# Softmax sums: adding four exponential tiles into one with accumulating transfers

## The chip, the cores and the metric

One core of a Trainium2 chip runs the kernel. The metric is the device time in microseconds of one execution; the median of several executions is given. The profile is of one execution of its own.

## The reference

Attention with an RMS norm on queries and keys, then two matrix products with a leaky ReLU between them. There are 8 batches, 12 heads, 448 positions and a head dimension of 64; the second part has 3584 rows, widths 768 and 2048.

```python
q_n, k_n = (rmsnorm(q, g_q), rmsnorm(k, g_k))
scores = scale * np.matmul(q_n, k_n.transpose(0, 1, 3, 2))
scores = scores - np.max(scores, axis=-1, keepdims=True)
attn = np.exp(scores)
attn = attn / (np.sum(attn, axis=-1, keepdims=True) + 1e-09)
return np.matmul(attn, v).astype(np.float32)
# with x = the above, its heads put side by side:
h = x @ w_in
g = np.maximum(0.01 * h, h)
return (g @ w_out).astype(np.float32)
```

## The kernel before, in words

The attention is cut into 24 units: unit u is four heads of one batch, three units to a batch. The key positions of a unit are cut into seven tiles. For each tile t, `score` (L195) writes the transposed scores to PSUM, keys on the partitions and the 448 queries along a row, and `ex` (L214, ScalarE) writes their exponentials as fp16 to the tile `et[:, t]`: 128 partitions, each with two rows of 448, 224 KB in all.

Since keys lie on partitions, the softmax sum of a query is a sum over partitions and over the seven tiles. For units 4 to 22 (`narrow`) TensorE does it in `zcol` (L283): a matrix of ones and zeros, 128 by 32, is the stationary operand, and each tile takes four matmuls of 224 columns that write four different groups of 32 PSUM partitions. Seven tiles accumulate in the same bank, 28 matmuls. From the sums ScalarE makes the inverse (`zcol_ln` L300, `zcol_inv` L305), four transfers of SyncE spread it over the partitions (L310, tile `rz`), and GpSimd multiplies it with the unit's unscaled output (`xmul_pool`, L320), for units up to 7 VectorE. `pv_out` (L295, ScalarE) has copied that output from PSUM to `x32`, of which there is one buffer.

The order of the work is written out by hand; each engine runs its instructions in that order. The main loop goes over the units, and each unit has four steps d = 0 to 3, which compute key tiles 0; 1 and 2; 3 and 4; 5 and 6. In step 0 of unit u TensorE does the scores of tile 0, then for unit u-1 the product with v (`pv_slot`, L340) and `zcol`, then `shift_mm` (L244), a small matmul that takes the maximum of unit u over partitions; VectorE made its input `dg` (L234) just before. L245 and L253 on VectorE turn it into the bias `eb` that every exponential of the unit needs. On ScalarE, `pv_out` of unit u-1 stands ahead of the first exponential of u.

The rest of each step is filled by `fill` from a queue of work on the two matrix products of earlier batches (L362, L403, L444, L564); the queue is spread so that it is empty when the next batch is ready. `load` brings q and k for unit u+4 on SyncE's queue. GpSimd's queue carries in step 0 the load of v for unit u+3 (`load_v`, L124), which waits for the end of unit u-1's product, and in step 1 `xmul_pool` of unit u-1.

Of the kernel before, what the change touches and what calls it, by code (L numbers as in the profile page):

```python
# [8 lines left out]
FP32 = mybir.dt.float32  # L9
FP16 = mybir.dt.float16  # L10
AF = mybir.ActivationFunctionType
ALU = mybir.AluOpType
# [6 lines left out]
def kernel(  # L19
# [11 lines left out]
    nc = tc.nc  # L31

    B, H, S, D = q.shape
    QH = 4
    NS = 7
    P = 128
    NQ = H // QH
    NU = B * NQ
# [6 lines left out]
    cst = ctx.enter_context(tc.tile_pool(name="cst", bufs=1))  # L45
# [4 lines left out]
    zpool = ctx.enter_context(tc.tile_pool(name="zpool", bufs=1))  # L50
# [6 lines left out]
    def aux(shape, dtype, name):  # L57
        if held:
            return held[0].pop(0)
        return psum.tile(shape, dtype, tag="aux", bufs=4, name=name)  # L60
# [6 lines left out]
    def drop(bank):  # L67
        if held:
            held[0].append(bank)
# [5 lines left out]
    onesr = cst.tile([P, 32], FP16)  # L75
# [6 lines left out]
    nc.vector.memset(eps_t, 1.0e-6)  # L82
    one32 = cst.tile([1, 1], FP32)
    nc.vector.memset(one32, 1.0)
    grow = cst.tile([1, 2, D], FP32)
    gdup = cst.tile([1, 2, D], FP32)
    gcol = cst.tile([P, 1], FP32)
    gate_t = cst.tile([P, 1], FP16)
    vts = [cst.tile([P, 2, NS, D], FP16, name=f"vt{i}") for i in range(NV)]
# [21 lines left out]
    st = {}  # L111
# [11 lines left out]
    def load_v(u):  # L123
        nc.gpsimd.dma_start(vts[u % NV].rearrange("p a t d -> p a (t d)"), rows(v, u))  # L124
# [9 lines left out]
    def buf(u, name):  # L134
        if name not in st[u]:
            shape, dtype, bufs = SHAPES[name]
            st[u][name] = prep_p.tile(shape, dtype, tag=name[:2] if bufs == 3 and name != "qkT" else name, bufs=bufs, name=name)
        return st[u][name]
# [7 lines left out]
    def prep_sqp(u, tis=BOTH):  # L146
        for ti in tis:
            nc.gpsimd.tensor_tensor(buf(u, f"sq{ti}"), raw[u][ti], raw[u][ti], op=ALU.mult)
# [49 lines left out]
    def qk(u, steps):  # L198
        st[u]["sT"] = []
        for t in steps:  # L200
            sT = slot()
            score(u, t, (sT[:, 0], sT[:, 1]))
            st[u]["sT"].append((t, sT))
# [17 lines left out]
    def shift_max(u):  # L221
        s = st[u]
        sT = s["sT"][0][1]
        if isinstance(sT, list):
            pm2 = small.tile([P, 2], FP32, tag="pm2", name="pm2")
            for a in range(2):
                nc.vector.tensor_reduce(pm2[:, a:a + 1], sT[a][:, 0:S], axis=AXL.X, op=ALU.max)
            s["spare"] = sT[0]
            nc.vector.tensor_reduce(s["spare"][:, 511:512], pm2, axis=AXL.X, op=ALU.max)
        else:  # L230
            s["spare"] = sT[:, 0]
            nc.vector.tensor_reduce(s["spare"][:, 511:512], sT[:, :, 0:S], axis=AXL.XY, op=ALU.max)  # L232
        s["dg"] = small.tile([P, P], FP16, tag="dg", name="dg")
        nc.vector.tensor_tensor(s["dg"], ident16, s["spare"][:, 511:512].broadcast_to([P, P]), op=ALU.mult)  # L234
# [20 lines left out]
    def gate(u):  # L255
        nc.gpsimd.tensor_copy(gate_t, buf(u, "n16")[:, 1, NS - 1, 1, D - 1:D])
# [11 lines left out]
    def zsum_slot(u):  # L268
        s = st[u]
        s["zslot"] = slot()  # L270
        s["zt"] = [s["zslot"][:, r] for r in range(2)]
        zsum(u)

    HS = S // 2

    def zcol(u):
        s = st[u]
        s["zc"] = aux([P, 512], FP32, "zc")
        for t in range(NS):
            for y in range(2):  # L280
                for a in range(2):
                    c = 32 * (2 * y + a)
                    nc.tensor.matmul(s["zc"][c:c + 32, 0:HS], onesr, s["et"][:, t, a, HS * y:HS * y + HS],  # L283
                                     start=(t == 0), stop=(t == NS - 1))

    def pv_slot(u):
        s = st[u]
        s["pslot"] = slot()
        s["pv"] = [s["pslot"][:, r] for r in range(2)]
        pv(u)  # L290

    def pv_out(u):
        s = st[u]
        s["x32"] = zpool.tile([P, 2, S], FP32, tag="x32", name="x32")
        nc.scalar.copy(s["x32"], s["pslot"][:, :, 0:S])  # L295

    def zcol_ln(u):
        s = st[u]
        s["zs"] = zpool.tile([P, HS], FP32, tag="zs", name="zs")
        nc.scalar.activation(s["zs"], s["zc"][:, 0:HS], AF.Ln)  # L300
        drop(s["zc"])

    def zcol_inv(u):
# [3 lines left out]
        for r in range(2):  # L307
            for y in range(2):
                src = s["zs"][64 * y + r:64 * y + 64:2, None, :]
                nc.sync.dma_start(s["rz"][:, r, HS * y:HS * y + HS], src.broadcast_to([32, 4, HS]))  # L310

    def xmul_sb(u):
        xmul_pool(u, nc.vector)

    def xmul_pool(u, eng=nc.gpsimd):
        s = st[u]
        b, g = divmod(u, NQ)
        if b not in xts:
            xts[b] = xpool.tile([P, NQ, 2, S], FP16, tag="xt", name="xt")
        eng.tensor_tensor(xts[b][:, g], s["x32"], s["rz"], op=ALU.mult)  # L320
# [375 lines left out]
    def narrow(u):  # L696
        return 4 <= u < NU - 1
# [46 lines left out]
    with tc.manual_schedule():  # L744
# [182 lines left out]
        for u in range(3, NU):  # L927
            for d in range(4):
                if d > 0 or u > 3:
                    qk(u, STEPS[d])  # L930
                    if d == 0:
                        shift_max(u)
                        if u == 6:
                            xmul_sb(u - 2)
                        if narrow(u - 1):
                            pv_slot(u - 1)
                            zcol(u - 1)
                            shift_mm(u)
                            pv_out(u - 1)
                        else:  # L940
                            zsum_slot(u - 1)
                            pv(u - 1)
                            shift_mm(u)
                            zinv(u - 1)
                    ex(u)
                    if d == 0 and narrow(u - 1):
                        zcol_ln(u - 1)
                jobs = []

                def job(fn, *args):  # L950
                    jobs.append(lambda: fn(*args))

                if d == 0:
                    if u == 3:
                        prep_norm(4)
                        gate(4)
                    elif narrow(u - 1):
                        if u < NU - 1:
                            job(zcol_inv, u - 1)
                    else:  # L960
                        xmul(u - 1)
                    if u + 4 < NU:
                        job(load, u + 4)
                    if u + 3 < NU:
                        load_v(u + 3)
                    if u < 6:
                        prep_sqp(u + 3)
                if d == 1 and narrow(u - 1) and not 5 <= u < 8 and u < NU - 1:
                    xmul_pool(u - 1)
                if u == NU - 1:  # L970
                    if d == 1:
                        job(zcol_inv, u - 1)
                    if d == 2:
                        xmul_pool(u - 1)
                if fed(u, d) and u > 3:
                    push(u // NQ - 1)
                if (u, d) in ((3, 1), (4, 0)):
                    for ti in range(2):
                        prep_tr(u + 1, ti, VV)
                if d == 1 and 5 <= u < NU - 1:  # L980
                    job(prep_g, u + 1)
                if u + 2 < NU:
                    if d == 1:
                        for ti in range(2):
                            job(prep_ssq, u + 2, ALL, (ti,))
                    if d == 2:
                        job(prep_rinv, u + 2)
                        for ti in range(2):
                            job(prep_norm, u + 2, ALL, (ti,))
                        if u > 3:  # L990
                            job(prep_trd, u + 2)
                if d == 1 and 4 <= u < 8:
                    job(weight_sum, u - 4, 0)
                if d == 0 and 5 <= u < 9:
                    job(weight_sum, u - 5, 1)
                if d == 2 and 6 <= u < 8:
                    job(xmul_sb, u - 1)
                if u == NU - 2 and d == 0:
                    for n, tile_ in ((1, (raws, "rq", 3)), (2, (raws, "rk", 3)), (3, None), (4, (prep_p, "sq", 3))):
                        job(win_sum, n, 1, tile_)  # L1000
                    for n in (3, 1, 2, 4):
                        job(x_sum, LATE, n)
                if d == 3 and 6 <= u < NU - 3:
                    for ti in range(2):
                        job(prep_sq, u + 3, ALL, (ti,))
                fill(u, d, jobs)
# [4 lines left out]
        for i, ns in enumerate(((3, 1), (2, 4))):  # L1011
            c, fn = queue[i]
# [33 lines left out]
```

## Time and profile before

| What | Value |
|---|---|
| median of 3 runs | 422.42 us (421.37 to 422.44) |
| profiled execution, its own time | 422.04 us |
| its span, first to last instruction | 420.3 us |
| mean granted clock of TensorE | 0.992 |
| TensorE busy | 404.4 us |
| ScalarE busy | 303.6 us |
| VectorE busy | 269.2 us |
| GpSimd busy | 83.0 us |
| moved by DMA | 62.42 MB, mean 149 GB/s |

PE is TensorE's matmuls and PEld its weight loads, DVE VectorE, ACT ScalarE, POOL GpSimd, SP SyncE. A row of a timeline gives the start in us, the length in us, engine, line, operation, the tiles written and read, and the count; in square brackets the idle time before it and what ended it. A "q" behind an engine's name is its queue of transfers. A transfer's landing is counted from its issue.

### The profile page before, as it was taken

Reading aid. Unit: us, or ns where it says so; the run is one execution under the profiler, and the core shown is the slowest. Engines: PE = TensorE matmul, PEld = TensorE weight load, DVE = VectorE, ACT = ScalarE, POOL = GpSimd, SP = SyncE. Lnnn points to the kernel's source line nnn. Section 1 sums busy time; section 2 is a strip of 40 time slices with the busy share of each in tenths; the row PEclk is TensorE's granted clock in tenths of the full one; section 3 lists DMA queues with packets and bytes.
Section 4 is the critical chain, followed back from the end, with each engine's and each line's share of the span. In section 5 each row is a group of like instructions: output and inputs, shape, how many; then the busy total and the mean of one; then the engine's idle time right before and its main releaser. Section 6 shows DMA issues by size and latency. Waiting matters only on the chain.

```text
span 420.3 us, 9568 instructions
## 1 busy us (share of the span) xinstructions
PE 404.4 (96%) x3959; PEld 222.9 (53%) x3959; DVE 269.2 (64%) x440; ACT 303.6 (72%) x474; POOL 83.0 (20%) x75
## 2 busy tenths in 40 slices
PE   7977999999999999999999999999999999999995
PEld 6544444555445544555445544455445557558853
DVE  5788665787658736466448745467338787527762
ACT  5999878868987689867986779967986657653600
POOL 1958422300020111210121111120101101010000
PEclk9699999999999999999999999999999999999999
DMA  8999999889664795678565796578562460032023
GB/s 257 218 239 237 235 250 147 200 156 215 169 153 68 224 212 120 168 163 180 152 130 107 194 203 150 151 141 170 180 111 44 121 155 11 7 78 75 2 53 100
DMA packets 71951, 62.42 MB, mean 149 GB/s; under 512 B 36324, under 2 KB 67044, under 8 KB 71908
## 3 DMA queue, kind: packets, MB, share of 16 engines
q1 hardware_dynamic: 61312, 49.62, 47.2%
q0 software_dynamic: 10272, 11.80, 18.1%
q8 instruction: 31, 0.51, 0.5%
q10 hardware_dynamic: 324, 0.39, 0.3%
q14 instruction: 12, 0.10, 0.1%
HBM read 45.61 MB, written 11.01 MB: 135 GB/s over the span
## 4 chain that ended last, share of the span: by engine, by line
PE 83%; ACT 8%; DVE 6%; issue 1%; DMA 1%; SPq 0%; DVEq 0%; ACTq 0%
PE hps L362 27%; PE sT L195 8%; PE sT L340 6%; PE ma L444 5%; PE md L444 5%; PE mc L444 5%; ACT et L214 5%; PE bank L444 5%; PE bank L564 4%; PE op L403 3%; PE zc L283 3%; PE mb L444 3%; DVE n L167 2%; PE sT L444 2%; PE bank L403 1%
## 5 line engine op out<-in xcount | busy, mean ns | idle before, releaser
L214 ACT ACTIVATE et<-sT,eb 128x896 f16<-128x896 f32 x166 | 159.4, 1010 | 18.6 <-PE sT L195 16.9
L362 PE MATMUL hps<-xt,win 128*128 128x448 f16 x600 | 120.8, 353 | 0.2 <-DVE xt L349 0.2
L362 PEld LDWEIGHTS <-win 128*128 128x128 f16 x612 | 56.8, 98 | 58.2 <-issue 9.6
L320 POOL TENSOR_TENSOR xt<-x,rz 128x896 f16<-128x896 f32 x16 | 33.4, 2085 | 148.0 <-DMA rz<-zs 139.5
L356 ACT ACTIVATE gt<-hps 128x448 f16<-128x448 f32 x100 | 54.0, 556 | 6.1 <-PE hps L362 5.4
L167 DVE TENSOR_TENSOR n<-rq,rinv 128x896 f16<-128x896 f32 (+2 forms) x25 | 27.2, 1090 | 47.0 <-ACT rinv L161 44.2
L195 PE MATMUL sT<-qkT 64*64 64x448 f16 x664 | 53.2, 369 | 3.0 <-ACT et L214 1.9
L155 DVE TENSOR_REDUCE ssq<-sq 128x14 f32<-128x896 f32 (+2 forms) x49 | 50.3, 1058 | 1.6 <-ACT sq L144 1.6
L444 PEld LDWEIGHTS <-sa 128*128 128x128 f16 x352 | 32.8, 98 | 26.3 <-issue 6.1
L295 ACT COPY x<-sT 128x896 f32<-128x896 f32 x19 | 17.2, 906 | 36.4 <-DVE sT L245 36.4
L124 POOL DMA_DIRECT2D vt<-in_v_dram x24 | 18.2, 757 | 114.9 <-PE sT L340 107.4
L444 PEld LDWEIGHTS <-gt 128*128 128x128 f16 x264 | 25.2, 98 | 18.7 <-issue 2.1
L195 PEld LDWEIGHTS <-qkT 64*64 64x64 f16 x672 | 15.2, 105 | 36.8 <-issue 33.5
L340 PE MATMUL sT<-et,vt 64*64 64x448 f16 x532 | 28.5, 350 | 0.3
L403 PE MATMUL op<-wout,gt 128*128 128x384 f16 x160 | 28.4, 327 | 0.0
L232 DVE TENSOR_REDUCE sT<-sT 128x1 f32<-128x896 f32 x22 | 24.1, 1093 | 4.3 <-PE sT L195 4.3
L340 PEld LDWEIGHTS <-vt 64*64 64x64 f16 x672 | 20.7, 107 | 11.3 <-issue 1.7
L167 DVE TENSOR_TENSOR n<-rk,rinv 128x896 f16<-128x896 f32 (+2 forms) x26 | 26.1, 1009 | 0.0
L403 PEld LDWEIGHTS <-gt 128*128 128x128 f16 x192 | 17.6, 98 | 14.3 <-issue 3.0
L444 PE MATMUL ma<-wout,gt 128*128 128x384 f16 x128 | 23.5, 326 | 0.0
L425 DVE TENSOR_TENSOR sa<-gt 128x512 f16<-128x512 f16 (+1 forms) x15 | 8.2, 544 | 18.5 <-ACT gt L356 13.9
L144 ACT ACTIVATE sq<-rq 128x896 f32<-128x896 f32 (+2 forms) x18 | 16.3, 913 | 1.3 <-DMA rq<-in_q_dram 1.3
(135 smaller groups left out, 516.6 us busy)
## 6 DMA issues: line engine op xcount, KB each, us to landing
rq<-in_q_dram SPq DMA_DIRECT2D x24, 448.0 KB, 3.9
rk<-in_k_dram SPq DMA_DIRECT2D x24, 448.0 KB, 5.6
out_dram<-ost SPq DMA_DIRECT2D x52, 192.0 KB, 3.3
rz<-zs SPq DMA_DIRECT2D x76, 112.0 KB, 2.3
vt<-in_v_dram POOLq DMA_DIRECT2D x24, 224.0 KB, 5.1
win<-in_moe_w_in_dram POOLq DMA_DIRECT2D x8, 384.0 KB, 16.8
wout<-in_moe_w_out_dram POOLq DMA_DIRECT2D x2, 1536.0 KB, 29.7
out_dram<-ost SPq DMA_DIRECT2D x4, 96.0 KB, 2.1
```

Of the source, the lines that this page charges most:

```text
L124: nc.gpsimd.dma_start(vts[u % NV].rearrange("p a t d -> p a (t d)"), rows(v, u))
L155: nc.vector.tensor_reduce(buf(u, "ssq")[:, ti, :, c[0]:c[1]], buf(u, f"sq{ti}")[:, :, c[0]:c[1]], axis=AXL.X, op=ALU.add)
L167: nc.vector.tensor_tensor(buf(u, "n16")[:, ti, c[0]:c[1]].rearrange("p s a d -> p a s d"), src[:, :, c[0]:c[1]], buf(u, "rinv")[:, ti, :, ...
L195: nc.tensor.matmul(banks[a][64 * r:64 * r + 64, 0:S].rearrange("p (t x) -> p t x", t=NS), kT(u, r, a, t), qT(u, r, a), start=True, stop=True)
L214: nc.scalar.activation(s["et"][:, t], sT[:, :, 0:S], AF.Exp, bias=s["eb"], scale=1.0)
L232: nc.vector.tensor_reduce(s["spare"][:, 511:512], sT[:, :, 0:S], axis=AXL.XY, op=ALU.max)
L320: eng.tensor_tensor(xts[b][:, g], s["x32"], s["rz"], op=ALU.mult)
L340: nc.tensor.matmul(s["pv"][r][64 * a:64 * a + 64, 0:S], vts[u % NV][64 * r:64 * r + 64, a, t], s["et"][64 * r:64 * r + 64, t, a], start=(t ...
L356: nc.scalar.activation(dst, src, AF.Prelu, bias=0.0, scale=1.0, alpha=0.01)
L362: nc.tensor.matmul(hps[:, 0:S], win16[:, kt // 2, kt % 2, ts(ft, P)], xt[:, kt // 2, kt % 2], start=(kt == 0), stop=(kt == KT - 1))
L403: nc.tensor.matmul(op2[:, 0:HC], gt[:, ft, ds(col(t), P)], wout16[:, ft, ds(HC * half, HC)], start=(ft == 0), stop=(ft == FT - 1))
L444: nc.tensor.matmul(bank[:, 0:HC], a[:, f], b[:, f], start=(first and f == 0), stop=(f == HF - 1), skip_group_check=not first)
```

## The change

For units 8 to 22 the first four exponential tiles are added into one fp16 tile, `ea`, by transfers that GpSimd issues: a plain copy of tile 0, and then accumulating transfers of tiles 1, 2 and 3. `zcol` then goes over tiles 4, 5 and 6 and over `ea`, which comes last: 16 matmuls for 28. `ea` has one buffer. On GpSimd's queue the copy stands in step 0 behind the load of v, the transfers of tiles 1 and 2 in step 1 ahead of `xmul_pool` of the unit before, that of tile 3 in step 2. The small tiles for the norm's gains, used at the start alone, lie in the buffer of `x32` now.

```diff
-    grow = cst.tile([1, 2, D], FP32)
-    gdup = cst.tile([1, 2, D], FP32)
+    g_t = zpool.tile([P, 2, S], FP32, tag="x32", name="g_t")
+    grow = g_t[0:1, 0, 0:2 * D].rearrange("p (a d) -> p a d", a=2)
+    gdup = g_t[0:1, 1, 0:2 * D].rearrange("p (a d) -> p a d", a=2)
...
+    NA = 4
+
+    def added(u):
+        return 8 <= u < NU - 1
+
+    def add_start(u):
+        s = st[u]
+        s["ea"] = zpool.tile([P, 2, S], FP16, tag="ea", name="ea")
+        nc.gpsimd.dma_start(s["ea"], s["et"][:, 0])
+
+    def add(u, t):
+        s = st[u]
+        nc.gpsimd.dma_start(s["ea"], s["et"][:, t], accum_op=ALU.add)
 
     def zcol(u):
         s = st[u]
         s["zc"] = aux([P, 512], FP32, "zc")
-        for t in range(NS):
+        ets = [s["et"][:, t] for t in range(NS)]
+        if added(u):
+            ets = ets[NA:] + [s["ea"]]
+        for t, e in enumerate(ets):
             for y in range(2):
                 for a in range(2):
                     c = 32 * (2 * y + a)
-                    nc.tensor.matmul(s["zc"][c:c + 32, 0:HS], onesr, s["et"][:, t, a, HS * y:HS * y + HS],
-                                     start=(t == 0), stop=(t == NS - 1))
+                    nc.tensor.matmul(s["zc"][c:c + 32, 0:HS], onesr, e[:, a, HS * y:HS * y + HS],
+                                     start=(t == 0), stop=(t == len(ets) - 1))
...
+                if added(u):
+                    if d == 0:
+                        add_start(u)
+                    if d == 1:
+                        add(u, 1)
+                        add(u, 2)
                 if d == 1 and narrow(u - 1) and not 5 <= u < 8 and u < NU - 1:
                     xmul_pool(u - 1)
+                if added(u) and d == 2:
+                    add(u, 3)
```

## The prediction

> **What bounds the kernel now.** I read the page first: span, busy time, and the chain that ended last.
>
> ```profile
> span 420.3 us, 9568 instructions
> PE 404.4 (96%) x3959; PEld 222.9 (53%) x3959; DVE 269.2 (64%) x440; ACT 303.6 (72%) x474; POOL 83.0 (20%) x75
> PE 83%; ACT 8%; DVE 6%; issue 1%; DMA 1%; SPq 0%; DVEq 0%; ACTq 0%
> ```
>
> TensorE carries 83% of the chain. The changed units run from about 115 to 358 us, so the windows view of that stretch comes next (busy time and count of each engine, clock, DMA share, GB/s).
>
> ```profile
> 115.00:358.00 243.00, 242.70 (x2332) 125.86 (x2334) 152.64 (x245) 187.71 (x294) 41.10 (x28) 1.00 0.63 143
> ```
>
> TensorE is filled for 242.70 of 243.00 us: whatever makes it wait here is added to the time, and whatever it is relieved of is taken off. The DMA engines are 0.63 busy and GpSimd nearly idle. Then the timeline around one head of a unit, unit 12, whose column sums for unit 11 start at 177.49.
>
> ```profile
> 177.49 0.60 PEld L283 LDWEIGHTS <-onesr 128*32 128x32 f16 x28 [0.36 <-issue]
> 177.49 0.85 PE L283 MATMUL zc<-et,onesr 128*32 128x224 f16 x28
> 177.86 0.29 DVE L234 TENSOR_TENSOR dg<-ident,sT 128x128 f16<-128x128 f16 x1
> 178.27 0.23 PE L244 MATMUL sT<-dg,onesp 128*128 128x64 f16 x2
> 178.93 0.91 ACT L295 COPY x<-sT 128x896 f32<-128x896 f32 x1 [1.27 <-DVE sT L245]
> 179.73 1.01 ACT L214 ACTIVATE et<-sT,eb 128x896 f16<-128x896 f32 x1
> ...
> 182.77 1.90 ACT L214 ACTIVATE et<-sT,eb 128x896 f16<-128x896 f32 x2 [1.36 <-PE sT L195]
> ...
> 186.03 1.91 ACT L214 ACTIVATE et<-sT,eb 128x896 f16<-128x896 f32 x2
> ```
>
> The 28 column-sum matmuls take 0.78 us (177.49 to 178.27). The maximum's matmul L244, the copy L295 and the first exponential L214 stand strictly behind them. Exponential tile 0 is done at 180.74, tile 1 at about 183.8, tiles 2 and 3 at 184.7 and about 187.0. The next unit's column sums start at 193.60. GpSimd's timeline over the same unit, and its transfers:
>
> ```profile
> 177.87 0.76 POOL L124 DMA_DIRECT2D vt<-in_v_dram  x1 [4.92 <-PE sT L340]
> 185.83 2.08 POOL L320 TENSOR_TENSOR xt<-x,rz 128x896 f16<-128x896 f32 x1 [7.21 <-DMA rz<-zs]
> 193.99 0.76 POOL L124 DMA_DIRECT2D vt<-in_v_dram  x1 [6.08 <-PE sT L340]
> ```
>
> ```profile
> DMA to landing us min/median/max: 3.5/5.1/28.8
> ```
>
> ```profile
> q1 hardware_dynamic: 43967, 31.49, 52.2%
> q0 software_dynamic: 3536, 2.98, 10.0%
> rz<-zs SPq DMA_DIRECT2D x60, 112.0 KB, 2.3
> vt<-in_v_dram POOLq DMA_DIRECT2D x13, 224.0 KB, 4.0
> ```
>
> The first of these is of all v loads, the second the DMA view of 114.9 to 357.8 us. A v load, GpSimd's only transfer there, lands 3.5 us after its issue at best and 4.0 in the middle.
>
> **What the Trainium skill says.** "DMA: Bandwidth & Descriptors", Anatomy of one DMA — SWDGE path: a transfer from GpSimd costs about 2.0 us fixed plus bytes over 436 GB/s, mostly completion, and a wait is served on the issuing sequencer. For 229,376 bytes that is an estimate of 2.5 us; the trace's 3.5 at best is longer, and it decides. Same page, Rules for kernel authors: an accumulate reads its destination and writes it later, so each must wait for the semaphore of the earlier one; no run here shows one yet, but it is why the four transfers cannot overlap. "Collectives: The Full Stack", The bandwidth ceiling: the add itself costs nothing, the second source read does. So an accumulate of 224 KB reads 448 KB and writes 224 KB: just the traffic of a v load (448 KB of fp32 in, 224 KB out), which makes the v load the nearest row.
>
> **The change part by part.**
>
> *Removed.* Units 8 to 22 run 16 column-sum matmuls instead of 28. Twelve go, 12/28 of 0.78 us or, as they run four at a time about 0.10 us apart, 0.29 us. It pays only if the next matmul can start earlier: L244 needs dg. In unit 12 dg ends at 178.15, 0.66 after the column sums start, so 0.07 remain. By the timelines of the fifteen heads dg ends 0.28 to 0.36 after that start in eleven, in the others at 0.49, 0.66, 0.66 and 0.80. The gain is 11 x 0.29 + 0.24 + 2 x 0.07 + 0 = 3.6 us, if nothing else changes.
>
> *Added on GpSimd and DMA.* Per unit one copy and three accumulates of 224 KB, 60 in all. Their issue, 0.76 us each as for v, is covered by GpSimd's idle time. Their length is not: copy, add 1, add 2, add 3 form a series, and the last four matmuls of the next column sums wait for its end.
>
> *The new loop.* Let s be the moment at which those last four are released (178.09 in unit 12, where the weight loads end). From s, tile 0 is ready after 180.74 - 178.09 = 2.65 us. The copy may then start, since the column sums that read the single buffer are over too. Its landing: between rz's 2.3 (half the size, another queue) and v's 3.5; I take 2.7, so with 0.1 to wake it is done at s + 5.45. Add 1 also needs tile 1, at s + 5.7 in unit 12 and 5.3 on the mean of the fifteen units; the later of the two gives about s + 5.6. The adds follow one another: tile 2 (6.6) and tile 3 (8.9) are there before. So the next release comes at 5.6 + 3 x (L + 0.1), L being one accumulate from issue to landing.
>
> *L.* Low: 3.0, a quiet v load less some of its HBM latency, as these sit in SBUF. High: 5.1, v's median over the whole run, heavy phases included. For longer: adds 1 and 2 meet the rz copies, stores and q/k loads, add 3 the DMA transpose and the stores at the end of a unit, and they bring traffic: at v's 10.0% x 243 / 13 = 1.9 us of all sixteen engines, three adds and a cheaper copy ask for 6.6 us per unit, beside 10.2 now (0.63 x 16.2). I take 4.2, somewhat over the stretch's 4.0.
>
> *The sum.* The fifteen units now take (357.82 - 114.90) / 15 = 16.19 us each (starts of their column sums). The loop takes 5.6 + 3 x 4.3 = 18.5, so 2.3 more; fifteen times 34.7 us. The saved matmuls give nothing here: TensorE only reaches the wait earlier. 420.3 + 34.7 = 455.0 us of span, plus the 1.7 that the profiled execution (422.04) has beyond it, is 456.7; the median of the runs (422.42) is 0.4 higher. Forecast 457.
>
> *Moved.* xmul (L320) of the unit before now stands behind add 2, hence starts at about s + 10.7, 188.8 instead of 185.83. Its readers, the first hps matmuls of a batch, come after the next head (TensorE is on the previous pair until 193.6), and the x buffer is rewritten at 195.04: some 3 us of cover, and the loop lengthens it. The v load stands behind add 3, but is for three units later. The exponentials' new waits on old transfers are two units late and free. The gain rows in another pool: an early, tiny load into a buffer first used at 74 us; free.
>
> **Rivals.** (a) *All hidden, faster*: if L stays at or under 3.3, the loop is at most 5.6 + 10.2 = 15.8, below 16.19 - 0.29, and the 3.6 us are gained: 420.3 - 3.6 + 1.7 = 418.4. For it: the sources sit in SBUF, quiet v loads take 3.5, and 0.37 of the DMA engines are free. Against: three in a row must all be quiet, and by the windows view 190 to 205 us is 0.83 busy. (b) *The DMA engines become the bound or the add is slow*: L of 5.1 gives 5.6 + 15.6 = 21.2, +5.0 a unit, 420.3 + 75 + 1.7 = 497; and waits of that length may lower TensorE's clock ("TensorE: Matmul & The Clock Gate", Part 1: half rate after an idle window of about 3.4 us; here the clock is 1.00 throughout the stretch and no run shows a drop there), so beyond 500. For it: 16.8 of 18.5 us of DMA time wanted, by the v load's price. Against: that price includes waiting. (c) *No difference*: L near 3.4, stalls and savings cancel: 422. A narrow strip. That the sums don't shorten is excluded: the column sums' program has 180 matmuls fewer.
>
> **How the numbers follow.** The forecast's case (L 3.5 to 5.1, own range 425 to 497) 0.73; (a) 0.13; (b) 0.11; (c) 0.03, of which 0.02 lie within 0.3% (1.3 us, about what a measurement can tell from no change) and 0.01 above. Slower: 0.73 + 0.11 + 0.01. Because each us of L is worth 45 us, the range is wide: 419, near (a)'s end, to 505, into (b).
>
> **What would show it.** Right: 16 column-sum matmuls, with a gap on TensorE before the last four that ends with a transfer into ea; heads about 18.5 us apart; accumulates landing 4.2 us after issue, each issued as the one before lands; GpSimd waiting on its own transfers. Wrong: heads 15.9 apart and no TensorE wait on ea (a), a PEclk below 1.0 or a DMA share near 1 (b), or add 3 waiting for xmul instead of add 2.

## The result and the profile after

The changed kernel takes 512.92 us (506.44 to 516.05) against 421.96 us: 1.2105 times as long, interval 1.1992 to 1.2219. The forecast was 457, its range 419 to 505. The direction and the place were right, the size was not. Medians are of all runs of a kernel; ratios leave out runs that lie more than 1.5% above its fastest. The profiled execution took 506.44 us, the shortest of the four; its span is 504.7 us, 84.4 more than before.

The page of the kernel after, in the same parts as shown of before (span, busy times, a row of the slices with the clock that TensorE was granted, and a group with its wait):

```profile
span 504.7 us, 9348 instructions
PE 425.7 (84%) x3779; PEld 226.8 (45%) x3779; DVE 289.8 (57%) x440; ACT 305.7 (61%) x474; POOL 131.5 (26%) x135
PEclk9799999999897989798898988799798999999999
L300 PE MATMUL zc<-ea,onesr 128*32 128x224 f16 x56 | 4.6, 314 | 60.5 <-DMA ea<-et 60.5
```

TensorE is 84% busy, and although it has 180 matmuls fewer, its busy time rose by 21 us. The last row says where it stood: 60.5 us of idle time ahead of the matmuls that read `ea`, all ended by the transfers into `ea`. (Another 69.7 us are listed ahead of the weight loads of the same line.) The sevens and eights in PEclk are new: before, it was nines from the third slice on. That is where the added busy time comes from, the same matmuls at a lower clock: by the trace TensorE was busy for 53.9 us at half clock, 6.1 before.

The tile view of `ea` gives the issues, the first and last reading, and the landings of all 60 transfers:

```profile
L300 PE MATMUL zc<-ea,onesr x56: 256/307/369, 136.1 to 422.3; 128*32 128x224 f16 x56
L288 POOL DMA_DIRECT2D ea<-et x45: 838/866/907, 121.3 to 436.9; - x45
L284 POOL DMA_DIRECT2D ea<-et x15: 568/581/590, 118.5 to 425.3; - x15
L300 PE MATMUL bank<-ea,onesr x4: 259/259/259, 442.8 to 442.8; 128*32 128x224 f16 x4
DMA to landing us min/median/max: 2.2/3.5/7.3
```

From the first release (the moment at which the last four column-sum matmuls start) at 136.1 to the last at 442.8 there are 14 loops: (442.8 - 136.1) / 14 = 21.9 us each, where units of 16.2 stood. Fifteen units with some 5.7 us more are the whole difference.

One loop in GpSimd's timeline, unit 12, from its release at 204.50 to the next at 225.63:

```profile
207.64 0.58 POOL L284 DMA_DIRECT2D ea<-et  x1 [4.75 <-ACT zs L317]
212.80 0.87 POOL L288 DMA_DIRECT2D ea<-et  x1 [4.58 <-ACT et L215]
218.23 0.87 POOL L288 DMA_DIRECT2D ea<-et  x1 [4.56 <-issue]
218.81 2.40 POOL L337 TENSOR_TENSOR xt<-x,rz 128x896 f16<-128x896 f32 x1
221.90 0.87 POOL L288 DMA_DIRECT2D ea<-et  x1 [0.69 <-ACT sq L145]
```

And TensorE's timeline around the same loop:

```profile
197.62 0.47 PE L300 MATMUL zc<-et,onesr 128*32 128x224 f16 x12
204.50 0.38 PE L300 MATMUL zc<-ea,onesr 128*32 128x224 f16 x4 [6.41 <-DMA ea<-et]
204.91 4.92 PE L420 MATMUL op<-wout,gt 128*128 128x384 f16 x16
...
225.63 0.28 PE L300 MATMUL zc<-ea,onesr 128*32 128x224 f16 x4 [2.84 <-DMA ea<-et]
```

The copy is issued 3.1 us after the release, add 1 at 8.3, add 2 at 13.7, add 3 at 17.4, and the column sums are released at 21.1. By the trace add 1 landed at 217.71 and add 2 was issued at 218.23: 0.52 us lie between. The 16 matmuls of L420 take 4.92 us here and took 2.76 in the same place before. The windows view of the wait, of the stretch behind it and of the next says why (the third figure from the end is the clock):

```profile
197.00:204.50 7.50, 1.09 (x29) 0.52 (x22) 3.28 (x3) 0.80 (x1) 3.03 (x3) 0.86 0.68 108
204.50:209.30 4.80, 4.80 (x20) 2.31 (x20) 1.66 (x4) 2.45 (x4) 0.58 (x1) 0.50 0.41 85
209.30:218.00 8.70, 8.70 (x68) 4.30 (x67) 5.42 (x8) 4.71 (x8) 0.87 (x1) 1.00 0.86 196
```

After a wait of 6.4 us TensorE works at half its clock for 4.8 us. The scores of tile 1 stand behind that work. ScalarE's timeline has the exponentials of tiles 1 and 2 in one row:

```profile
211.49 1.91 ACT L215 ACTIVATE et<-sT,eb 128x896 f16<-128x896 f32 x2 [3.49 <-PE sT L196]
```

They start 6.99 us after the release; in the same unit of the kernel before it was 4.68 (182.77 - 178.09). So tile 1, and add 1 with it, come late.

### The profile page after: what moved, and what is told of

It reads as the page before. It is cut to its first block, busy times and chain, and to the rows that moved or that the text cites. A ratio compares the mean times of both kernels' runs of the same rounds, so it can differ in the third digit from the quotient of the medians.

```text
span 504.7 us, 9348 instructions
## 1 busy us (share of the span) xinstructions
PE 425.7 (84%) x3779; PEld 226.8 (45%) x3779; DVE 289.8 (57%) x440; ACT 305.7 (61%) x474; POOL 131.5 (26%) x135
## 5 line engine op out<-in xcount | busy, mean ns | idle before, releaser
L379 PE MATMUL hps<-xt,win 128*128 128x448 f16 x600 | 134.0, 380 | 0.2 <-DVE xt L366 0.2
L379 PEld LDWEIGHTS <-win 128*128 128x128 f16 x612 | 60.7, 104 | 67.7 <-issue 25.4
L288 POOL DMA_DIRECT2D ea<-et x45 | 39.0, 867 | 152.5 <-ACT et L215 79.8
L373 ACT ACTIVATE gt<-hps 128x448 f16<-128x448 f32 x100 | 54.4, 550 | 18.6 <-PE hps L379 17.4
L300 PE MATMUL zc<-ea,onesr 128*32 128x224 f16 x56 | 4.6, 314 | 60.5 <-DMA ea<-et 60.5
L337 POOL TENSOR_TENSOR xt<-x,rz 128x896 f16<-128x896 f32 x16 | 38.7, 2418 | 17.3 <-DMA rz<-zs 17.3
L300 PEld LDWEIGHTS <-onesr 128*32 128x32 f16 x352 | 8.4, 96 | 69.7 <-issue 69.7
L168 DVE TENSOR_TENSOR n<-rk,rinv 128x896 f16<-128x896 f32 (+2 forms) x26 | 39.0, 1508 | 0.0
L246 DVE TENSOR_REDUCE sT<-sT 128x1 f32<-128x128 f32 x19 | 5.7, 299 | 56.0 <-PE sT L245 56.0
L461 PEld LDWEIGHTS <-gt 128*128 128x128 f16 x264 | 26.3, 102 | 20.9 <-issue 5.7
L420 PE MATMUL op<-wout,gt 128*128 128x384 f16 x160 | 32.1, 356 | 0.0
L284 POOL DMA_DIRECT2D ea<-et x15 | 8.7, 579 | 78.7 <-ACT zs L317 73.0
L420 PEld LDWEIGHTS <-gt 128*128 128x128 f16 x192 | 18.8, 104 | 16.5 <-issue 6.3
```

The costliest lines, as they stand in the source:

```text
L168: nc.vector.tensor_tensor(buf(u, "n16")[:, ti, c[0]:c[1]].rearrange("p s a d -> p a s d"), src[:, :, c[0]:c[1]], buf(u, "rinv")[:, ti, :, ...
L288: nc.gpsimd.dma_start(s["ea"], s["et"][:, t], accum_op=ALU.add)
L373: nc.scalar.activation(dst, src, AF.Prelu, bias=0.0, scale=1.0, alpha=0.01)
L379: nc.tensor.matmul(hps[:, 0:S], win16[:, kt // 2, kt % 2, ts(ft, P)], xt[:, kt // 2, kt % 2], start=(kt == 0), stop=(kt == KT - 1))
L420: nc.tensor.matmul(op2[:, 0:HC], gt[:, ft, ds(col(t), P)], wout16[:, ft, ds(HC * half, HC)], start=(ft == 0), stop=(ft == FT - 1))
L461: nc.tensor.matmul(bank[:, 0:HC], a[:, f], b[:, f], start=(first and f == 0), stop=(f == HF - 1), skip_group_check=not first)
```

## Experiments

Two theories at first. *Series*: the time goes into four transfers that wait for one another, at the end of which TensorE waits. *Traffic*: 13.8 MB more on the DMA engines slow everything. The fifteen runs, each beside runs of the kernel before on its own chip (421.6 to 422.3 us):

| Run | median us | ratio, interval |
|---|---|---|
| sums_only | 419.1 | 0.9943 (0.9921 to 0.9964) |
| two_tiles | 421.7 | 0.9994 (0.9977 to 1.0011) |
| before_three_out | 428.3 | 1.0158 (1.0133 to 1.0183) |
| before_early | 441.8 | 1.0468 (1.0431 to 1.0506) |
| gpsimd_adds | 447.4 | 1.0611 (1.0584 to 1.0638) |
| three_tiles | 460.7 | 1.0884 (1.0815 to 1.0953) |
| quiet_queue | 464.4 | 1.0999 (1.0959 to 1.1039) |
| traffic_no_wait | 465.1 | 1.0941 (1.0861 to 1.1021) |
| two_series | 465.3 | 1.1012 (1.0942 to 1.1081) |
| no_loads | 472.9 | 1.1172 (1.1139 to 1.1205) |
| late_read | 474.0 | 1.1240 (1.1213 to 1.1267) |
| early_tile1 | 489.0 | 1.1601 (1.1550 to 1.1653) |
| keep_clock | 505.6 | 1.1862 (1.1785 to 1.1939) |
| keep_clock_mid | 512.3 | 1.2035 (1.1962 to 1.2108) |
| keep_clock_long | 516.0 | 1.2109 (1.2038 to 1.2181) |

### sums_only: the gain by itself

```diff
         if added(u):
-            ets = ets[NA:] + [s["ea"]]
+            ets = ets[NA:] + ets[:1]
...
-                    if d == 0:
-                        add_start(u)
-                    if d == 1:
-                        add(u, 1)
-                        add(u, 2)
...
-                if added(u) and d == 2:
-                    add(u, 3)
```

> No transfers; the column sums of units 8 to 22 take tiles 4, 5, 6 and 0 alone, 16 matmuls; tiles 1 to 3 are left out of the sums. Both theories: 418 to 419 us, the 3.6 us that the prediction worked out for the shorter sums. If it stays at 422, the sums were never worth anything at this place.

419.1 against 421.8, a gain of 2.7 us, 0.6%. The 3.6 us of the prediction were of the right kind and somewhat large. This is about all that the shorter sums could have brought here.

### traffic_no_wait: the transfers without TensorE's wait

```diff
-            ets = ets[NA:] + [s["ea"]]
+            ets = ets[NA:] + ets[:NA]
```

> All 60 transfers are issued as in the changed kernel, but the column sums of units 8 to 22 take all seven exponential tiles again (28 matmuls), so TensorE waits for no transfer. Theory 'series' (the time goes into TensorE's wait at the end of four serial transfers): nearly all of the 91 us goes, 422 to 437 us; above 422 only if the series, some 17 us a unit on GpSimd's queue, is itself longer than a unit of 16.2 us and holds xmul back. Rival 'traffic' (the 13.8 MB more that the DMA engines move[...] slow the rest): 480 us or more.

465.1 us, between the two. The series acts even when no matmul reads its result. From the waits view of ScalarE (us in total, times, longest):

```profile
ACT x L312 <- POOL xt L337: 43.5, 7, 10.8
```

The timeline of GpSimd around the head of unit 11, at 163:

```profile
169.71 0.88 POOL L288 DMA_DIRECT2D ea<-et  x1 [3.33 <-issue]
170.28 2.40 POOL L337 TENSOR_TENSOR xt<-x,rz 128x896 f16<-128x896 f32 x1
...
177.13 0.58 POOL L284 DMA_DIRECT2D ea<-et  x1 [2.12 <-DMA ea<-et]
```

and ScalarE's timeline at the same place:

```profile
172.72 0.91 ACT L312 COPY x<-sT 128x896 f32<-128x896 f32 x1 [8.85 <-POOL xt L337]
```

GpSimd's queue is in order. The traced execution took 465.97 us; its units take (464.1 - 420.3) / 15 + 16.2 = 19.1 us, and so do the copies by the trace. The series is longer than a unit of 16.2, so it falls behind until the multiplication of the unit before, queued behind add 2, is so late that ScalarE cannot copy the next output into the one `x32` buffer; the first exponential stands behind that copy. The 43.5 us of this wait are about the 43 us lost. So what costs is less the bytes by themselves than the series' length, by a back door that the prediction had dismissed with "some 3 us of cover". That the series is 19 us long is another matter, and there traffic comes in.

### three_tiles and two_tiles: a shorter series

```diff
-    NA = 4
+    NA = 3
...
-                if added(u) and d == 2:
-                    add(u, 3)
```

> Only tiles 0, 1 and 2 are added (copy and two accumulates), the column sums run 20 matmuls. Theory 'series': the series ends about 5.6 + 0.3 + 5.3 + 0.5 + 4.1 = 15.8 us after the release, just inside a unit of 16.2 us, so the clock stays up and the time is 419 to 428 us. Rival 'traffic': three quarters of the traffic and of the loss, about 490 us.

460.7 us, some 33 us above what was expected of the series. The waits view of the traced execution (465.69 us) has TensorE still waiting. By the trace, on the mean of the last 14 units, add 1 is issued at 7.64 instead of 5.9 and the two accumulates take 5.3 and 4.8 us, so the series ends at 18.3, past the unit.

```profile
PE zc L300 <- DMA ea<-et: 25.0, 8, 5.1
```

two_tiles also sets `NA = 2` and leaves out `add(u, 2)`.

> Only tiles 0 and 1 are added, one copy and one accumulate a unit, 24 matmuls. Theory 'series': lands at 5.6 + 0.3 + 5.3 = 11.2 us after the release, five us ahead of its reader: 420 to 422 us, the gain of one group of four matmuls at most 1.4. Rival 'traffic': half of the loss, about 465 us.

421.7 us, no difference. Its transfers are no shorter than in the others, up to 7.1 us, by the tile view of `ea`:

```profile
L300 PE MATMUL zc<-ea,onesr x56: 259/259/259, 132.3 to 340.0; 128*32 128x224 f16 x56
...
who waited for it (us, times):
  POOL ea L288: 2.6, 1
...
DMA to landing us min/median/max: 2.2/4.1/7.1
```

but two in a row end before their reader, by 0.8 us at the least and 4.2 on the mean of the last 14, so TensorE waits for none of them. Half the traffic by itself costs nothing here, where half of the loss was expected of it; the gain of one group of four matmuls, 1.4 us at most, does not show.

### late_read: the wait moved off the exponentials

```diff
...
+            if added(u) and (t == len(ets) - 1) != (part == 1):
+                continue
...
+                    late = added(u - 1)
+                    if d == 1 and late:
+                        zcol(u - 1, 1)
                     ex(u)
-                    if d == 0 and narrow(u - 1):
+                    if (d == 0 and narrow(u - 1) and not late) or (d == 1 and late):
                         zcol_ln(u - 1)
...
+                if d == 1 and added(u - 1):
+                    zcol_inv(u - 1)
...
```

> All four tiles are added and read, but the last four column-sum matmuls (those on ea), the inverse and its spreading stand one step later, in step 1 of the next unit, behind the first exponential. Theory 'series': the first exponential and step 0 no longer wait, the loop is the bare series, about 2.3 + 5.3 + 4.1 + 3.8 + 4 x 0.5 = 17.5 us, 1.5 a unit over before: 440 to 450 us. Rival 'traffic': same transfers, same loss, about 510 us.

474.0 us. Step 0 no longer waits and 39 us come back, but a unit takes (471.3 - 420.3) / 15 + 16.2 = 19.6 us, not 17.5, and TensorE waits in seven units:

```profile
PE zc L303 <- DMA ea<-et: 26.9, 7, 7.7
```

By the trace, on the mean of the last 14 loops, 18.3 us lie between the reading of `ea` and the last landing of the next series: 1.0 till the copy is issued, 4.0 for the copy, 3.2, 4.2 and 4.3 for the accumulates, 1.7 between them. The other 1.6 us pass between the landing and the reading. So this is not the bare series alone, though that too is longer than a unit. Together with traffic_no_wait: about half of the 91 us is a series longer than a unit, the other half comes from closing it through the first exponential, so that it cannot start before it has ended. This split is read from the two runs; no run separates the halves cleanly.

### no_loads and quiet_queue: what makes the transfers long

```diff
     def load(u, engines=None):
+        if u >= 12:
+            raw[u] = raw[9 + u % 3]
+            st[u] = {}
+            return
```

> The changed kernel without the loads of q and k for units 12 to 23, which use the rows of units 9 to 11 again. If contention with these loads makes the first and second accumulate long (5.3 and 4.1 us on the mean, 3.1 where the queue is quiet): they fall to about 4 and 3.3, the loop by 2 us, 480 to 490 us. If the accumulates are long by themselves: 505 us or more.

472.9 us, 40 less than the changed kernel and below what was expected. By the trace the means of the three accumulates over the last 14 loops fall from 5.40, 4.10 and 3.70 us to 3.95, 3.54 and 4.03, the loop from 21.9 to 19.8.

quiet_queue leaves out the DMA transposes of these units too:

```diff
     def prep_trd(u):
+        if u >= 12:
+            st[u]["qkT"] = st[u - 3]["qkT"]
+            return
```

> The changed kernel without the loads of q and k and without the DMA transposes of the normed q and k for units 12 to 23, which use the rows of units 9 to 11 and their transposed tiles again; stores, rz copies and v loads stay. If what SyncE's queue moves at the same time is what makes the accumulates longer than the 3.1 us of the quiet ones: all three near 3.3 us, the loop 5.6 + 0.3 + 3 x 3.3 + 2 x 0.53 = 16.9 us instead of 21.8, no more clock dips, 425 to 440 us. If the loads were all of it: as no_loads, 470 us.

464.4 us, not 425 to 440. Add 3 falls to 3.42, add 2 to 3.40, but add 1 stays at 3.99, it is issued at 6.98 and not at 5.9, and the loop is 19.2. So the transfers that were taken away account for 2.4 of the 3.9 us that the three accumulates took beyond 3.1 each, the loads for 1.7 of them. That the rest comes from the rz copies and stores, which stay, is likely but not tested. Of the 2.3 us by which the loop missed its estimate, 1.1 are the start of add 1, the term on which the prediction failed too, and 0.9 the accumulates.

### two_series: the same transfers, half as long a series

```diff
...
-            ets = ets[NA:] + [s["ea"]]
+            ets = ets[NA:] + [s["ea"], s["eb2"]]
...
-                        add(u, 2)
+                        add_start(u, 2, "eb2")
...
-                    add(u, 3)
+                    add(u, 3, "eb2")
```

> The same 60 transfers and bytes, but as two short series: tile 1 is added to a copy of tile 0, tile 3 to a copy of tile 2 in a second buffer, and the column sums read both (20 matmuls). To make room the output staging has three buffers instead of four. Theory 'series' (each transfer waits for the one before, 17 to 19 us in all): the last one is issued after tile 3, at about 10.5 us after the release, and lands at 15, inside a unit of 16.2: 419 to 430 us. Rival 'traffic' (the bytes themselves slow the transfers and the rest): about as slow as the changed kernel, 490 us or more.

465.3 us. Its control has `bufs=3` for `opool` and nothing else:

> The kernel before with three buffers for the output staging instead of four, as two_series has them. If that alone explains the waits of two_series on its score matmuls (four of about 3 us): some 435 us, and two short series cost about 30 us rather than 43. If it costs nothing: 422 us, and the whole of two_series' loss is its own.

428.3 us, so 37 of the 43 us are two_series' own. GpSimd's timeline in unit 10 shows it:

```profile
159.68 0.87 POOL L288 DMA_DIRECT2D ea<-et  x1 [4.65 <-ACT et L215]
160.24 0.87 POOL L284 DMA_DIRECT2D eb<-et  x1
160.81 2.41 POOL L337 TENSOR_TENSOR xt<-x,rz 128x896 f16<-128x896 f32 x1
166.81 0.89 POOL L288 DMA_DIRECT2D eb<-et  x1 [3.60 <-ACT sq L145]
```

The two series' transfers now run beside each other and beside the loads: by the trace the accumulate and the copy land 6.0 us after issue each, and the last one is issued at 166.81, after the next head has begun. In unit 20, with no loads left, they took 3.42 and 3.15, and the series ended in time. Here traffic does cost, by lengthening a series; how much of it is the loads and how much the other series, this run does not tell.

### keep_clock, keep_clock_long, keep_clock_mid: the clock

```diff
+            if added(u) and t == len(ets) - 1:
+                for x in range(64):
+                    nc.tensor.matmul(s["pslot"][:, x % 2, S:S + 64], onesp, onesp[:, 0:64], start=True, stop=True)
```

> The changed kernel with 64 dummy matmuls of 64 columns (some 3.5 us, no use made of their result) put on TensorE ahead of the last four column-sum matmuls, where it waits for ea anyway, so that it is not idle for long. If the clock dips lengthen the loop (tile 1 is ready 1.5 us later after a wait than in the kernel before): clock back to 0.97 or more, tile 1 at 5.3 us after the release, 490 to 500 us. If the dips only stand in time that the wait covers: 510 us or more.

505.6 us, its runs between 498.0 and 516.0. The clock still dips in nine of the 14 loops of the profiled execution (515.98 us).

`range(144)` in place of `range(64)`:

> As keep_clock, with 144 dummy matmuls (the 64 took 2.04 us by its trace, not 3.5, so the wait was still long and the clock still dipped; 144 take 4.6). If the dips are what makes tile 1 late after a wait (6.8 us after the release on the mean, 4.4 in the units without a dip): clock 0.98 or more, tile 1 at about 5.3, the loop 1.5 us shorter, 485 to 495 us. If not: 500 us or more.

516.0 us. Clock 0.982, tile 1 at 5.55 us instead of 6.88 (means of 14 loops), add 3 landed at 20.86 instead of 21.68, but the loop stayed 21.9: in several loops the dummies held TensorE past the last landing, and accumulates got longer (13.5 against 13.2 us in all). Unit 12, released at 198.99, shows what a full clock does: the clock of the 4.8 us behind the release, and the exponentials of tiles 1 and 2:

```profile
198.99:203.79 4.80, 4.80 (x42) 2.60 (x40) 2.64 (x6) 2.54 (x5) 0.58 (x1) 1.00 0.58 118
203.70 1.91 ACT L215 ACTIVATE et<-sT,eb 128x896 f16<-128x896 f32 x2 [1.35 <-PE sT L196]
```

They start 4.71 us after the release, as in the kernel before (4.68).

`range(104)`:

> As keep_clock, with 104 dummy matmuls, 3.3 us. If tile 1's delay comes from the clock dips and sets the loop: few dips, tile 1 at about 5.6 us after the release, no release held by a dummy, the loop 20.7 us (where the 144 had the last transfer landed), 495 to 500 us. If the time that tile 1 gains is lost again to longer transfers: 508 us or more.

512.3 us, clock 0.956: the dips were still there in half of the loops. In the traces of the three runs, 23 of 42 loops have the full clock between the release and tile 1, and in all 23 tile 1 is ready within 0.02 us of its time in the same unit of the kernel before. In the 19 with a dip it is 0.9 to 2.9 us later. So the dips make tile 1 late. The dummies do not show what that is worth: none of the three reached the time expected of it.

### early_tile1: tile 1 early by another order

```diff
-    WD = (3.6, 2.9, 2.8, 2.8)
+    WD0 = (3.6, 2.9, 2.8, 2.8)
+    WD1 = (1.2, 3.7, 3.6, 3.6)
+
+    def WD(u):
+        return WD1 if 9 <= u < NU - 1 else WD0
...
-        debt[0] += total * WD[d] / left
+        debt[0] += total * WD(u)[d] / left
```

> The changed kernel with less filling work in step 0 of units 9 to 22 and more in steps 1 to 3, so that the scores of tiles 1 and 2 come some 2.4 us sooner after the release, dip or not. If tile 1's lateness is worth what it is late: the first accumulate starts when the copy has landed, at about 5.6 instead of 7.25, the loop is 20.2 us, 485 to 495 us. If it is given back: 505 us or more.

489.0 us, as expected. The tile view gives the loops, (425.4 - 135.4) / 14 = 20.7 us:

```profile
L300 PE MATMUL zc<-ea,onesr x56: 255/270/370, 135.4 to 404.5; 128*32 128x224 f16 x56
L300 PE MATMUL bank<-ea,onesr x4: 259/259/259, 425.4 to 425.4; 128*32 128x224 f16 x4
```

Tile 1 is ready at 4.54, add 1 issued at 6.39 instead of 7.36. It cannot be issued earlier, since now the copy holds it: issued at 3.11, landed 2.74 later, and 0.54 from there to the next issue. The control, the kernel before with the same shift:

> The kernel before with the same shift of filling work, as the control: 421 to 426 us if the shift costs nothing or little by itself; what it costs is to be taken off early_tile1.

441.8 us: the shift costs 20 us where TensorE is the bound, much more than expected, and still gains 24 in the changed kernel by the medians, 17.9 by the spans of the profiled executions (1.2 us a loop, of which 1.0 is the earlier issue of add 1). So some 18 to 24 us of the 91 hang on the lateness of tile 1. That nothing of the control's 20 us has to be set against them is argued from TensorE's wait, which covers the shift, and not measured.

### gpsimd_adds: the same sum without transfers

```diff
...
-        nc.gpsimd.dma_start(s["ea"], s["et"][:, t], accum_op=ALU.add)
+        if t == 1:
+            s["ea"] = zpool.tile([P, 2, S], FP16, tag="ea", name="ea")
+        nc.gpsimd.tensor_tensor(s["ea"], s["et"][:, 0] if t == 1 else s["ea"], s["et"][:, t], op=ALU.add)
...
-                    if d == 0:
-                        add_start(u)
```

> The same sum of four tiles and the same 16 matmuls, but GpSimd itself adds (three tensor_tensor of 128x896 fp16 a unit, no transfers), as each tile gets ready. If the length of the series is the cause: about 2.1 us an add as for xmul, the last one done some 12 to 14 us after the release, no wait on TensorE, no more DMA traffic: 419 us, as with the short sums alone. If GpSimd's reads hold VectorE up: 425 us or more.

447.4 us. The wait on `ea` is gone (1.3 us in all), but another took its place. GpSimd's adds in the tile view of `ea`:

```profile
L285 POOL TENSOR_TENSOR ea<-ea,et x30: 1878/2063/2807, 121.9 to 375.9; 128x896 f16<-128x896 f16 x30
```

VectorE's product with the norm's inverse, in the groups view, before and here:

```profile
L167 DVE TENSOR_TENSOR n<-rk,rinv 128x896 f16<-128x896 f32 (+2 forms) x26 | 26.1, 1009 | 0.0
L168 DVE TENSOR_TENSOR n<-rk,rinv 128x896 f16<-128x896 f32 (+2 forms) x26 | 42.6, 1643 | 0.0
```

and TensorE's timeline behind one such add, with the sum of these waits from the waits view:

```profile
203.33 0.22 PE L245 MATMUL sT<-dg,onesp 128*128 128x64 f16 x2 [1.08 <-DVE dg L235]
PE sT L245 <- DVE dg L235: 17.1, 13, 2.9
```

VectorE's norm products take 1643 ns on the mean, 1009 before; the maximum comes late, and L245 waits for `dg`, 17.1 us of the 25 lost. That GpSimd's adds slow VectorE fits what "SBUF — State Buffer" of the Trainium skill says in Who interferes with whom, that a VectorE instruction with two SBUF inputs contends with a GpSimd instruction that reads SBUF. The trace agrees: the eleven of these 26 products that ran beside a product or add of GpSimd took 2577 ns on the mean, the other 15 took 959. No version that computes the whole result beats the kernel before by more than can be measured.

## Why the prediction was wrong

**Right:** TensorE as the bound; the removal worth some 3 us (2.7 in sums_only); four transfers in series, the last released by a landing, the first exponential behind it; the loop from release to release as the thing to sum; the saved matmuls giving nothing.

**L, mis-sized a little.** Forecast 4.2 us each, 12.6 in all; measured 5.40 + 4.10 + 3.70 = 13.2, so 0.6 us a loop. The v load was a fair row. What it hides is the spread, 3.1 in a quiet queue and 7.3 at most, which follows SyncE's transfers (no_loads, quiet_queue).

**The 0.1 us to wake, mis-sized.** From landing to the next issue on GpSimd it is 0.53 to 0.59 us. From the last landing to the reading it is 0.04 in 13 of the 14 loops; the last loop, where the reading comes 2.69 after the landing, makes the mean 0.23. Behind the copy these gaps are 1.3 us instead of 0.3, 1.0 us a loop.

**The start of add 1, mis-sized most: the step that failed.** "The later of the two gives about s + 5.6": add 1 was issued at 7.36, 1.8 us later, for two reasons. First, the copy's own path is longer. It is issued at 3.17 and not at 2.75, lands at 5.82, and 0.53 pass to the next issue, so that add 1 could start at 6.35 at the earliest: 0.75 us. Second, the prediction took tile 1's 5.3 us from a kernel whose TensorE never waits. Behind a wait the clock halves, the filling work ahead of tile 1's scores takes longer, and tile 1 is ready at 6.88: another 1.0 us. The loops with and without a dip in the keep_clock runs show that the clock is the cause, and early_tile1, with add 1 at 6.39, shows that this part counts in time. The clock was in the text, but only as an addition to rival (b), for waits near 5 us. In the changed kernel twelve of the 14 loops have a dip, behind waits of 2.1 to 7.9 us.

Together 18.5 + 0.6 + 1.0 + 1.8 = 21.9, the loop measured. Summed by cause, the hand-overs (from tile 0 to the copy, from one transfer to the next, from the last landing to the reading) make up about 1.7 us of the 3.4, the clock 1.0 and L 0.6. Over the fifteen units that takes the 455.0 of span to the 504.7 measured. The range failed for the same reason: it varied L alone, and held every other term of a sum that is multiplied by fifteen at one value.

**Moved work.** xmul's cover was enough in the changed kernel, since the loop lengthens it. It was not enough as soon as the loop was opened (traffic_no_wait).

**Rivals.** (a) was never near: no loop was as short as 15.8 us. (b)'s time and its clock were right, by another route: the DMA engines were not full (share 0.70 over the stretch), and the adds not slow in themselves. A unit's four transfers took some 4.9 us of all sixteen engines and not 6.6, an estimate from the DMA view of 136 to 443 us (29.2% of 307 us for GpSimd's queue, less eleven v loads at 1.9, over 14 loops). The two mechanisms, a longer series and a lower clock, are not separate cases; the one brings the other.

**Open:** what the dips are worth in time by themselves; the dummies that were to show it moved other terms. And what an accumulate still takes beyond 3.1 us when the loads and transposes are gone.

## What to carry to other kernels

Four dependent transfers for a third of a microsecond of matmuls are a bad trade where the result is due within one stage: sum issue, landing and the gap to the next issue for every link, and compare with the stage before looking at bytes. Here the gaps between transfers, taken as 0.1 us and measured at 0.53, were by cause the largest part of the error. If such a series ends in a wait on an in-order engine that also starts the next series, it is a loop, and each term is paid every round. Take a term's duration from a state like the one forecast: TensorE, once it had to wait, came back at half its clock in twelve of 14 loops.

## What the hardware showed that was not expected

- An accumulating transfer of 224 KB from SBUF to SBUF takes 3.1 us in a quiet queue, a plain copy 2.2; beside the transfers of SyncE's queue the accumulate took up to 7.3 in the changed kernel, without the loads 6.5 at most and without the transposes too 5.8. The prediction took over from what its page states of a collective's add that the add itself costs nothing and the second read does. Here the accumulate takes 0.9 us more than the copy, and no run tells the two apart.
- From a landing to the issue of the transfer that waits for it on GpSimd's queue 0.53 us pass, five times the time supposed.
- TensorE's granted clock was 0.50 for 4.8 us after a wait of 6.4 us; sixteen matmuls took 4.92 us instead of 2.76. "TensorE: Matmul & The Clock Gate" of the Trainium skill, Part 1, puts the half rate after an idle window of about 3.4 us. The trace agrees on the rate, but four of the twelve loops with a dip had waits of only 2.1 to 2.8 us, and one wait of 3.0 us brought none. The release of unit 14, its wait and the clock behind it:

```profile
246.19 0.28 PE L300 MATMUL zc<-ea,onesr 128*32 128x224 f16 x4 [2.08 <-DMA ea<-et]
246.19:250.99 4.80, 4.80 (x21) 2.11 (x21) 0.46 (x2) 3.14 (x6) 0.58 (x1) 0.64 0.84 157
```

- GpSimd's multiplication took 2418 ns on the mean in the changed kernel and 2085 before, and VectorE's `n<-rk` 1508 and 1009: once xmul had moved, the two met. The ten `n<-rk` that ran beside it took 2374 ns on the mean, the other 16 took 967.
